# Sync loads the first keys and queries back to back, ScalarE the first values, in a new written order

## The chip, the cores and the metric

One core of a Trainium2 chip. Five instruction queues work side by side: TensorE (PE), VectorE (DVE), ScalarE (ACT), GpSimd (POOL) and sync (SP), which only issues transfers. Each runs its own queue in order. Time is device microseconds (us), median of the runs.

## What is computed

Sparse causal attention for 4 batches of 8 heads (768 positions, 64 values each), followed by a gated feed-forward layer. For each query and each chunk of 32 keys an upper bound is made from the chunk's smallest and largest key values; the six chunks with the highest bounds are kept.

```python
k_min, k_max = np.min(k_chunks, axis=3), np.max(k_chunks, axis=3)
ub = np.sum(np.maximum(q[..., None, :] * k_min, q[..., None, :] * k_max), axis=-1)
ub = np.where(causal, ub, -1e9)
top_chunks = np.argsort(ub, axis=-1)[..., -6:]
scores = np.where(sel & (i >= j), scale * q @ k.T, -1e9)
out = softmax(scores) @ v                       # (4, 8, 768, 64) -> x (3072, 512)
y = (1 / (1 + np.exp(-(x @ w_gate))) * (x @ w_val)) @ w_out   # 512 -> 1536 -> 512
```

All tensors are float32 in memory; the matmuls are in float16, besides the transposes and the bounds.

## The kernel before

The work is cut into nine stages: 128 positions of batch 0 (stage 0), the next 256 (stage 1), then seven of 384. A stage has three parts.

- Preparation: keys and queries are brought to the layout with the 64 values in partitions. For batch 0 (`prep_groups`) TensorE transposes each block of 128 positions (operations `kTp` and `qT`, line 561), DVE reduces the keys to chunk maxima and minima (`kxn`, line 571), four small DVE operations make the bounds' operand `kcat` (`kc`, lines 580 to 591), ScalarE and DVE evict the transposed keys (`hk`, line 604) and queries (`Qc`, line 522 and 526), and the queries are cast to `headQ` (`hq`, line 537). For the later batches (`prep_blocks`) DVE transposes. From stage 1 on TensorE makes the upper bounds (`ub`, line 733), and a serial chain on DVE turns them into mask rows: transpose (`ubq`, 736), causal penalty (741), the eight largest of each row (`mx`, 749), comparison (`Ap`, 754), transpose (`apT`, 757); the rows are copied beneath the queries in `headQ` (`mq`, 761), once for heads 0 to 3 and once for heads 4 to 7. Stage 0 has at most four chunks, so all are kept; it has only a guard against overflow (`ubp` line 699, guard 704 to 706, `gT` 708 and 712), and its keys and queries lie in `firstK` and `first`, with a pattern `less` copied into `firstK` (387).
- Attention: scores (`sc`, 810), exponential (`at`, 815, ScalarE), the causal triangle cut out by GpSimd (821), product with the values and a column of ones (`pv`, 835), normalisation by DVE (`xn`, 846 and 848), transpose (`xtp`, 861; `xT`, 866).
- Feed-forward: two products (`gv`, 891), `gate` on ScalarE (901), `hglu` on DVE (903), the output product (`o`, 917), its copy (`osb`, 924 or 926) and the store (932).

The order of all this is written out. The string `ORDER` names each of 1771 operations once, as kind, stage and number; `/1` or `/2` picks another of the engines that may do it. `Plan.order` walks through it with assumed durations and landings, only to find where TensorE would wait, and puts matmuls on zeros there (line 340, `fill`). On each engine the operations stand in the string's order. The same assumed times were used when the string was searched for; on the chip only the order, the engines and the number of fillers are left of them.

The first transfers stand in the table `LOADS`: lane, load, and assumed landing. The name of a load is tensor, stage and block: k10 is the keys of stage 1, block 0, 256 KB in pieces of 2 KB (line 455); v00a and v00b are the values of stage 0 for heads 0 to 3 and 4 to 7, 128 KB each in pieces of 256 B, and v10 and v11 are 256 KB each in the same pieces (line 460). Lane SP is sync's queue, Q2 is ScalarE's and Q0 is GpSimd's. `WLAND` has the assumed landings of the nine weight loads, which GpSimd issues (lines 507 and 509) with conversion to float16. GpSimd (or ScalarE) then casts the values of stages 0 and 1 into the tile `v` (line 491). p10 and p01 are copies of a pattern inside the on-chip memory (line 407). From stage 3 on keys and queries come in pieces of 128 B by sync (`kb` and `qb`, line 422).

Transfers issued by sync and ScalarE use eight completion semaphores in turn: a ninth waits until the first has landed. Six buffers are shared by all loads of keys, queries and values of this kind.

Of the kernel before, what the change touches and what calls it, by code (L numbers as in the profile page):

```python
# [20 lines left out]
ORDER = """
    c.0 kch.0 wst0.0 is.0 is.2 qch.0 c.2 w0.0 wst1.0 is.1 vn.0 c.3 vn.1 c.4 c.8/1 v.0 wst2.0 c.5 kTp:0.0 c.6 kch.1
    vn.2 qT:0.0 kxn:0.0 ps.0 kxn:0.1 Qc:0.1 qch.1 kc:0.0 wst3.0 w1.0 Qc:0.3 wst4.0 Qc:0.2 kch.2 hk:0.0 wst5.0 Qc:0.0
    hk:0.1 wst6.0 ubp:0.1 qch.2 hk:0.2/1 ubp:0.0 v.1 kTp:1.0 hk:0.3/1 c.9 qT:1.0 kxn:1.0 Ap:0.1 c.11 c.10 kxn:1.1
    Qc:1.1 wst7.0 w2.0 vn.3 gT:0.1/1 Qc:1.2/1 kTp:1.1 gT:0.0/1 sc:0.1 Qc:1.0/1 sc:0.0 at:0.2 kxn:1.3 Qc:1.3 at:0.3
    kxn:1.2 at:0.0 kc:1.0 qT:1.1 at:0.1 Qc:1.6 pl.0 hk:1.1 wst8.0 pv:0.3 pv:0.2 pv:0.6 pv:0.0 pv:0.1 Qc:1.4 xn:0.0
    w3.0 c.7 Qc:1.7 hk:1.2 xtp:0.0 pv:0.4 pv:0.7 pv:0.5 Qc:1.5 xn:0.1 hk:1.0/1 ub:1.0 Ap:0.0 xtp:0.1 ubq:1.0 hq:1.1
    xT:0.0/1 ubq:1.1 xT:0.1/1 mx8:1.0 hk:1.3/1 gv:0.6 kch.3 v.2 gv:0.0 qch.3 gv:0.7 Ap:1.0 hq:1.0/1 gv:0.1 w4.0 ub:1.1
    gv:0.8 kch.4 apT:1.0 gv:0.3 gv:0.2 gate:0.1 mq:1.3/2 v:0.0 ubq:1.2 sc:1.3 gate:0.0 mq:1.1 qch.4 ubq:1.3 at:1.6
    mx8:1.1 mq:1.0 sc:1.1 mq:1.2 gv:0.4 at:1.2 gv:0.5 Ap:1.1 sc:1.2 kch.5 at:1.4 sc:1.0 at:1.7 apT:1.1 mq:1.7/2 at:1.0  # L30
    mq:1.6/2 sc:1.7 mq:1.4/2 v.3 hglu:0.0 gv:0.9 gv:0.10 qch.5 at:1.14 sc:1.6 w5.0 at:1.3 pv:1.7 gv:0.11 at:1.1
    at:1.12 sc:1.4 at:1.5 pv:1.6 pv:1.1 mq:1.5 at:1.8 pv:1.4 pv:1.3 pv:1.2 pv:1.5 at:1.13 sc:1.5 xn:1.1 pv:1.0 at:1.9
    qT:2.0 at:1.10 at:1.15 hglu:0.1 kTp:2.0 c.13 at:1.11 xn:1.0 pv:1.14 gv:0.12 Qc:2.2 w6.0 gv:0.18 vn.4 gv:0.19
    gv:0.20 kxn:2.1 gv:0.13 c.14 gate:0.3 gv:0.14 vn.5 pv:1.9 pv:1.15 kxn:2.0 pv:1.13 gate:0.2 pv:1.10 pv:1.12 kTp:2.2
    vn.6 xn:1.3 Qc:2.0 kb:3.0 pv:1.8 pv:1.11 qT:2.2 xn:1.2 hk:2.0/1 xtp:1.0 w7.0 Qc:2.8/1 gv:0.15 Qc:2.3 gv:0.21
    xtp:1.1 xT:1.0 hk:2.1/1 gv:0.22 gv:0.23 xT:1.1 gv:0.16 gv:0.17 Qc:2.1 gv:1.0 hglu:0.2 kTp:2.1 gate:1.0 hglu:0.3
    gv:1.2 Qc:2.11 w8.0 kxn:2.2 gv:1.1 Qc:2.9 gv:1.4 hglu:1.0 gate:1.1 qT:2.1 kxn:2.5 gate:1.2 gv:1.12 Qc:2.6 kxn:2.4
    gv:1.3 gv:1.13 gate:1.6 hglu:1.1 Qc:2.5 gv:1.16 hglu:1.6 gv:1.5 kxn:2.3 gate:1.8 gv:1.10 Qc:2.10 gv:1.11 hglu:1.2
    Qc:2.4 gv:1.14 kc:2.0 gv:1.17 gate:1.5 hq:2.0 Qc:2.7 gv:1.18 hglu:1.5 hglu:1.8 gate:1.7 ub:2.0 v.4 gate:1.9 gv:1.6
    ubq:2.0 gv:1.19 kb:3.1 gate:1.3 ubq:2.1 ub:2.1 hk:2.2/1 mx8:2.0 o:0.0 kb:3.2 gv:1.7 hk:2.4/1 v.5 o:0.1 Ap:2.0  # L40
    hk:2.3/1 o:0.2 kb:3.3 o:0.3 apT:2.0 hk:2.5/1 o:0.4 mq:2.0/2 qb:3.0 v.6 o:0.5 hglu:1.9 mq:2.1 ubq:2.2 sc:2.0 mq:2.3
    gv:1.15 qb:3.1 hq:2.1 osb:0.0/1 at:2.0 sc:2.1 hglu:1.3 gv:1.20 at:2.2 qb:3.2 hglu:1.7 sc:2.3 at:2.1 ubq:2.3
    gv:1.21 mx8:2.1 gate:1.10 gv:1.8 qb:3.3 at:2.5 sc:2.2 Ap:2.1 gv:1.9 kb:3.4 gate:1.4 gv:1.22 mq:2.2 hglu:1.10
    at:2.3 sc:2.6 apT:2.1 kb:3.5 gv:1.23 gate:1.11 Qct:3.0 at:2.4 sc:2.4 at:2.9 pv:2.0 mq:2.4 kb:3.6 pv:2.4 pv:2.3
    hglu:1.4 pv:2.2 v:0.1 pv:2.1 at:2.6 sc:2.7 Qct:3.1 mq:2.5 kb:3.7 o:1.6 at:2.10 at:2.11 sc:2.5 kTt:3.0 vn:3.0
    pv:2.5 qb:3.4 o:1.7 at:2.8 xn:2.0 pv:2.11 at:2.7 sc:2.9 qb:3.5 mq:2.6 o:1.8 hglu:1.11 at:2.14 sc:2.8 mq:2.7 o:1.0
    qb:3.6 vn:3.1 at:2.12 pv:2.8 pv:2.9 pv:2.10 kTt:3.1 pv:2.7 sc:2.10 qb:3.7 rl:3.0 at:2.13 o:1.1 kn:3.0 c.12 o:1.9
    hq:3.0 kb:5.0 pv:2.6 pv:2.12 pv:2.13 at:2.15 sc:2.13 pv:2.14 kx:3.0 o:1.10 at:2.20 out:0.0 at:2.16 sc:2.12 kb:5.1
    o:1.11 at:2.18 sc:2.14 xn:2.1 o:1.2 at:2.21 o:1.3 kb:5.2 Qct:3.2 o:1.4 osb:1.1 sc:2.11 kc:3.0 o:1.5 at:2.17 kb:5.3
    sc:2.15 Qct:3.3 at:2.19 ub:3.0 at:2.23 at:2.22 pv:2.19 pv:2.17 qb:5.0 osb:1.0/1 pv:2.16 hk:3.0 pv:2.15 rl:3.1  # L50
    pv:2.20 pv:2.18 ubq:3.0 pv:2.22 pv:2.21 pv:2.23 xtp:2.0 xn:2.2 qb:5.1 hq:3.1 xT:2.0/1 xn:2.3 ubq:3.1 xtp:2.1
# [954 lines left out]
```

## Time and profile before

| | |
|---|---|
| median of 3 runs | 300.29 us (300.08 to 301.04) |
| the profiled execution | 300.8 us, span 298.8 us |
| TensorE busy | 284.5 us, 95% of the span |
| DVE, ScalarE, GpSimd busy | 71%, 68%, 36% |
| granted TensorE clock | 1.00 throughout |
| read from and written to memory | 28.31 MB and 6.29 MB |

The chain of work that ended last is TensorE for 83% of its length and DVE for 8%; 4% of the span is one transfer of queries. A row of the timeline gives start, length, engine, line, operation with its output and input, and in brackets how long the engine had been idle and what ended this. SPq and ACTq rows are the issue of a transfer, not the transfer.

### The profile page before, as it was taken

The numbers are of one execution on the slowest core, as the hardware profiler recorded it, in microseconds if no ns is written. First come the engines' busy times: TensorE is split into PE (matmuls) and PEld (weight loads), VectorE is DVE, ScalarE is ACT, GpSimd is POOL, SyncE is SP. The second block draws the span as 40 slices with busy tenths as digits, with TensorE's granted clock in tenths as the row PEclk, the third lists the DMA queues.
The fourth block names the chain that finished last, engine by engine and source line by source line (L and its number), as shares of the span: only waits on it lengthen the run. The fifth ranks groups of instructions, "written<-read, shape, count | busy, mean of one in ns | idle before, by whom it ended". The sixth has DMA issues, their size and how long they took to land.

```text
span 298.8 us, 6823 instructions
## 1 busy us (share of the span) xinstructions
PE 284.5 (95%) x2642; PEld 181.2 (61%) x2642; DVE 212.4 (71%) x581; ACT 203.9 (68%) x299; POOL 107.5 (36%) x175
## 2 busy tenths in 40 slices
PE   6668998999999999999999999999999999999995
PEld 3345983865665566566655656766665676555563
DVE  0688788998999898899988886897875434202431
ACT  3578896899786598887995886999636476331221
POOL 7567703685568143273851104326220101000000
PEclk9999999999999999999999999999999999999999
...
GB/s 152 256 218 279 229 171 114 193 149 175 74 215 160 43 141 58 96 63 109 111 85 2 124 0 2 3 3 71 20 70 2 35 2 0 2 103 39 0 70 106
DMA packets 110072, 27.99 MB, mean 94 GB/s; under 512 B 100311, under 2 KB 105525, under 8 KB 110040
## 3 DMA queue, kind: packets, MB, share of 16 engines
q1 hardware_dynamic: 81608, 19.28, 31.5%
...
q10 hardware_dynamic: 1712, 0.66, 1.1%
q8 instruction: 20, 0.33, 0.5%
q14 instruction: 12, 0.10, 0.1%
HBM read 28.31 MB, written 6.29 MB: 116 GB/s over the span
## 4 chain that ended last, share of the span: by engine, by line
PE 83%; DVE 8%; DMA 4%; ACT 2%; issue 1%; SPq 1%; DVEq 0%; ACTq 0%
PE m_o L917 21%; PE m_v L891 17%; PE m_g L891 16%; PE big_sc L810 12%; PE m_pv L835 6%; PE big_gv L891 5%; PE m_ub L733 4%; DMA ld_q<-in_q_dram 4%; PE m_xtp L861 2%; ACT Qcat L522 1%; DVE kxn L571 1%; DVE mx L749 1%; PE big_kqT L561 1%; ACT at L815 1%; DVE hglu L903 1%
## 5 line engine op out<-in xcount | busy, mean ns | idle before, releaser
L815 ACT ACTIVATE at<-big_sc 128x1024 f16<-128x1024 f32 (+3 forms) x96 | 84.7, 909 | 17.1 <-PE big_sc L810 11.6
L917 PE MATMUL m_o<-wo,hglu 128*128 128x512 f16 (+1 forms) x300 | 72.0, 370 | 0.0
L821 POOL TENSOR_SCALAR_AFFINE_SELECT at<-at 128x384 f16<-128x384 f16 (+2 forms) x66 | 33.3, 515 | 105.5 <-ACT at L815 101.6
L891 PE MATMUL m_v<-xT,wv 128*128 128x384 f16 (+2 forms) x384 | 71.2, 306 | 0.1
L891 PE MATMUL m_g<-xT,wg 128*128 128x384 f16 (+2 forms) x384 | 70.3, 306 | 0.0
L903 DVE SCALAR_TENSOR_TENSOR hglu<-gate,m_v 128x384 f16<-128x384 f16 (+1 forms) x88 | 44.9, 527 | 19.8 <-PE m_v L891 15.5
L901 ACT ACTIVATE gate<-m_g 128x384 f16<-128x384 f32 (+1 forms) x88 | 40.8, 477 | 24.4 <-PE m_g L891 20.3
L891 PEld LDWEIGHTS <-wg 128*128 128x128 f16 x432 | 38.7, 98 | 23.8 <-issue 4.4
L810 PE MATMUL big_sc<-headQ,headK 89*128 89x128 f16 (+2 forms) x472 | 51.6, 240 | 0.8 <-DVE headQ L761 0.6
L891 PEld LDWEIGHTS <-wv 128*128 128x128 f16 x432 | 38.6, 98 | 20.6 <-issue 0.9
L810 PEld LDWEIGHTS <-headK 89*128 89x128 f16 x472 | 33.4, 97 | 12.7 <-issue 1.1
L917 PEld LDWEIGHTS <-hglu 128*128 128x128 f16 x300 | 27.0, 98 | 22.7 <-issue 1.2
L835 PEld LDWEIGHTS <-at 128*128 128x128 f16 x672 | 30.2, 98 | 12.7 <-issue 1.9
L835 PE MATMUL m_pv<-v,at 128*128 128x65 f16 x672 | 34.0, 194 | 1.1 <-POOL at L821 1.1
L761 POOL COPY headQ<-apT 25x384 f16<-25x384 f16 (+1 forms) x30 | 14.7, 490 | 27.1 <-DVE apT L757 25.6
L672 DVE STREAM_TRANSPOSE Qcat<-ld_qb 64x768 f32<-64x768 f32 x24 | 23.1, 964 | 0.8 <-POOL headQ L537 0.4
L924 ACT ACTIVATE osb<-m_o 128x512 f32<-128x512 f32 (+1 forms) x17 | 9.9, 587 | 18.7 <-PE m_o L917 18.7
L903 DVE SCALAR_TENSOR_TENSOR hglu<-gate,big_gv 128x384 f16<-128x384 f16 x12 | 6.6, 553 | 21.9 <-ACT gate L901 20.7
L848 DVE TENSOR_TENSOR xnat<-m_pv,rz 128x384 f16<-128x384 f32 (+1 forms) x34 | 18.1, 534 | 1.2
L537 POOL CAST headQ<-Qcat 64x1536 f16<-64x1536 f32 (+1 forms) x11 | 15.6, 1419 | 8.8 <-ACT Qcat L522 8.6
L901 ACT ACTIVATE gate<-big_gv 128x384 f16<-128x384 f32 x12 | 5.9, 491 | 17.4 <-PE big_gv L891 17.4
L681 ACT ACTIVATE Qcat<-Qcat 64x1536 f32<-64x1536 f32 x11 | 16.3, 1483 | 0.3
...
## 6 DMA issues: line engine op xcount, KB each, us to landing
...
wv<-in_moe_w_val_dram POOLq DMA_DIRECT2D x3, 512.0 KB, 15.0
...
```

The lines of the kernel that those rows point to most:

```text
L537: copy(tl(("headQ", s), [89, H, st.n], F16)[0:64, h0:h0 + 4, :], tl(("Qcat", s))[0:64, h0:h0 + 4])
L672: nc.vector.transpose(tl(qd, [128, H, HS])[0:64, h:h + 2].rearrange("p a (c t) -> p a c t", t=CH), tl(("ld", "qb", b, u))[64 * e:64 * e + ...
L681: nc.scalar.activation(dst, src, AF.Relu)
L810: nc.tensor.matmul(ps[:, 128 * o:128 * (o + m)], (hk if s else firstK)[0:rows, h, jl:jl + 128], (tl(("headQ", s)) if s else first)[0:rows, ...
L815: add(at(x + 0.03 * t + 0.01), [("ACT", 0.19 + w * 0.815e-3, lambda sc=sc, a=a, w=w: nc.scalar.activation(tl(a, [128, 1024], F16)[:, 0:w], ...
L821: nc.gpsimd.affine_select(out=dg, in_=dg, compare_op=ALU.is_ge, fill=0.0, base=0, pattern=[[0, nd], [1, 128]], channel_multiplier=-1)
L835: nc.tensor.matmul(pvp[:, ib - q0, h % HP, :], tl(a)[:, 128 * o:128 * o + 128], head_v(b, jb // HB)[:, h, jb % HB, :], start=(jb == 0), st ...
L848: nc.vector.tensor_tensor(dst, pvp[:, :, :, 0:64], r.to_broadcast([128, nb, HP, 64]), ALU.mult)
L891: nc.tensor.matmul(ps(i)[:, n * (fb - f0):n * (fb - f0 + 1)], w16[:, c, 128 * fb:128 * fb + 128], tl(("xT", s, c // 2))[:, c % 2, :], star ...
L901: add(at(x) - EV, [("ACT", 0.18 + 0.81 * el, lambda gate=gate, ps=ps: nc.scalar.activation(tl(gate, [128, G * n], F16), ps(0), AF.Tanh, sc ...
L903: add(at(x) - EV, [("DVE", 0.15 + 1.04 * el, lambda gate=gate, hg=hg, ps=ps: nc.vector.scalar_tensor_tensor(tl(hg, [128, G * n], F16), tl( ...
L917: nc.tensor.matmul(tl(o, [128, N]), tl(("hglu", s, fc // G))[:, c0:c0 + 128], wo16[:, fc, cols], start=(fc == 0), stop=(fc == NFB - 1))
```

## The change

Two tables and the order string change, and a third table is new; `Plan.order` reads it. No operation is added or taken away.

```diff
 LATENCY = {"PE": 0.22, "ACT": 0.08, "DVE": 0.06, "POOL": 0.12, "SP": 3.0, "Q0": 3.0, "Q2": 3.0}
+BEGIN = {"DVE": 0.9, "ACT": 0.8, "POOL": 1.3}
...
-        end, eng_of, free, used, released, rings = {}, {}, {}, {}, {}, {p: [] for p in self.slots}
+        end, eng_of, free, used, released, rings = {}, {}, dict(BEGIN), {}, {}, {p: [] for p in self.slots}
...
-    WLAND = [9.6, 15.0, 18.9, 23.5, 28.6, 32.0, 35.1, 38.2, 44.6]
-    LOADS = (("SP", "k00", 4.8), ("Q2", "q00", 4.8), ("SP", "v00a", 8.0), ("Q2", "v00b", 8.0), ("SP", "k10", 10.1), ("SP", "q10", 11.7),
-             ("SP", "k11", 13.3), ("SP", "q11", 16.0), ("Q2", "v10", 17.4), ("SP", "v11", 23.8),
-             ("SP", "k20", 24.0), ("SP", "q20", 25.0), ("SP", "k21", 26.2), ("SP", "q21", 27.8), ("SP", "k22", 29.3), ("SP", "q22", 32.5),
-             ("SP", "p10", 33.7), ("SP", "p01", 35.0), ("Q0", "v20", 46.0), ("Q0", "v21", 46.5), ("Q0", "v22", 47.0))
+    WLAND = (11.7, 15.3, 19.3, 24.0, 28.5, 32.6, 35.8, 39.0, 45.4)
+    LOADS = (("SP", "k00", 4.8), ("SP", "q00", 6.1), ("Q2", "v00a", 5.0), ("Q2", "v00b", 5.5), ("SP", "k10", 8.0), ("SP", "q10", 9.4),
+             ("SP", "k11", 10.8), ("SP", "q11", 13.0), ("Q2", "v10", 13.8), ("SP", "v11", 21.2),
+             ("SP", "k20", 22.7), ("SP", "q20", 24.2), ("SP", "k21", 25.7), ("SP", "q21", 27.2), ("SP", "k22", 28.7), ("SP", "q22", 30.2),
+             ("SP", "p10", 31.4), ("SP", "p01", 32.8), ("Q0", "v20", 46.0), ("Q0", "v21", 46.5), ("Q0", "v22", 47.0))
```

The times in these tables are assumptions of the kernel's author for the planner, not measurements of this text. `ORDER` is replaced as a whole. Its beginning before and after (`wst` is the issue of a weight load, `is` an issue by ScalarE, `kch`, `qch` and `vn` loads of keys, queries and values, `c` a constant, `v:` or `v.` a cast of values):

```diff
-    c.0 kch.0 wst0.0 is.0 is.2 qch.0 c.2 w0.0 wst1.0 is.1 vn.0 c.3 vn.1 c.4 c.8/1 v.0 wst2.0 c.5 kTp:0.0 c.6 kch.1
-    vn.2 qT:0.0 kxn:0.0 ps.0 kxn:0.1 Qc:0.1 qch.1 kc:0.0 wst3.0 w1.0 Qc:0.3 wst4.0 Qc:0.2 kch.2 hk:0.0 wst5.0 Qc:0.0
...
+    kch.0 is.0 c.0 wst0.0 is.1 vn.0 qch.0 c.2 is.2 w0.0 wst1.0 kch.1 c.3 vn.1 vn.2 c.4 v.0 kTp:0.0 wst2.0 qch.1 c.5
+    kxn:0.0 qT:0.0 c.6 kch.2 kxn:0.1 Qc:0.0 c.8 qch.2 ps.0 kTp:1.0 Qc:0.2 kc:0.0 wst3.0 Qc:0.3 qT:1.0 wst4.0 Qc:0.1
...
```

What that makes of each queue at the start, in issue order:

| queue | before | after |
|---|---|---|
| sync | k00, v00a, k10, q10, k11, q11, v11, k20, ... | k00, q00, k10, q10, k11, q11, v11, k20, ... |
| ScalarE, transfers | q00, v10, v00b | v00a, v00b, v10 |
| ScalarE, then | `less` into `firstK`, 4 `Qc` of stage 0, 2 `headK` copies, 1 `Qc` of stage 1, both `gT` copies, exponentials | 4 `Qc` of stage 0, 4 `Qc` of q10, 1 `gT` copy, both exponentials, 4 `Qc` of q11 |
| DVE | `kxn`, `kc`, `hk` of stage 0, guard, 2 `kxn`, 2 `Qc`, 2 `kxn`, `kc`, `hk` | `kxn`, `less`, `kc`, `hk` of stage 0, guard, `kxn`, 1 `gT` copy, 3 `kxn`, `hk`, `kc`, `hk` |
| GpSimd | ..., wg, wv, wg, wv (third), wo, cast of v00, ..., wo, masks of stage 0, wo | ..., wv, wg (third), cast of v00, wv (third), memset, 2 `headK` copies and the pattern `pen` with a wo issue between, masks of stage 0, wo, wo |
| TensorE | k00, q00, fillers, `ubp`, k10, q10, `gT`, k11, scores, q11, `pv` | k00, q00, k10, q10, `ubp`, k11, `gT`, q11, scores, fillers, `pv` |

In the whole program TensorE has 13 fillers fewer. On GpSimd the two `headQ` casts of stage 2 (line 537) stand directly behind each other, where mask-row copies stood between; the two of stage 1 are both on ScalarE. Behind stage 2 the order has the same structure, with heads and blocks exchanged here and there and some copies on another of the three engines.

More of the change, by code (lines that the diff above doesn't have):

```diff
@@ L25 @@
[L25 to L49, printed above, removed]
@@ new lines @@
+    ubq:4.0 kb:7.3 o:2.8 ubq:4.1 o:2.9 mx8:4.0 pv:3.23 o:2.10 o:2.11 Ap:4.0 pv:3.20 pv:3.21 pv:3.5 osb:2.1 pv:3.4
+    ub:4.1 apT:4.0 pv:3.19 pv:3.3 pv:3.22 pv:3.18 out:2.1 o:2.12 ubq:4.2 mq:4.0/1 pv:3.0 pv:3.2 pv:3.1 o:2.13 out:2.0
+    mq:4.1/1 xn:3.3 o:2.14 mq:4.2/1 sc:4.1 xn:3.0 xtp:3.1 at:4.2 o:2.15 ubq:4.3 mx8:4.1 xtp:3.0 sc:4.0 xT:3.1/1 o:2.16
+    kTt:5.0 xT:3.0/1 o:2.17 sc:4.3 Ap:4.1 osb:2.2 gv:3.4 gv:3.5 at:4.0 out:2.2 gv:3.6 kTt:5.1 gv:3.8 qb:7.0 gv:3.9
+    gate:3.1 sc:4.4 apT:4.1 at:4.5 gv:3.7 Qct:5.1 mq:4.5 gv:3.16 gv:3.17 qb:7.1 hk:5.0 mq:4.3/1 sc:4.2 hglu:3.1
```

208 lines of the change are left out of this document (114 added, 94 removed).

## The prediction

> **What bounds the kernel now.** I read the page's busy table, then TensorE's busy time by stretch, then the same for its filler matmuls alone (line 340, on zeros), then the first 50 us of the timeline.
>
> ```profile
> PE 284.5 (95%) x2642; PEld 181.2 (61%) x2642; DVE 212.4 (71%) x581; ACT 203.9 (68%) x299; POOL 107.5 (36%) x175
> 0.00:30.00 30.00, 21.30 (x169) 1.00 1.07 227
> 30.00:45.00 15.00, 14.68 (x200) 1.00 1.37 197
> 45.00:50.00 5.00, 3.60 (x33) 1.00 0.93 105
> 60.00:291.00 231.00, 230.54 (x2116) 1.00 0.44 65
> 0.00:30.00 30.00, 11.23 (x45) 4.46 (x45) 1.00 1.07 227
> ```
>
> The columns of a stretch are its length, busy time (instructions), granted clock, DMA share and GB/s; the last row is filler alone. TensorE is the bound: 284.5 us of 298.8, never throttled (1.00). Of its busy time 11.23 us is filler, all before 30 us. Time without useful matmuls: 30 - (21.30 - 11.23) = 19.9 us before 30 us, 0.3 us from 30 to 45, 1.4 us from 45 to 50, 0.5 us in the 231 us from 60 to 291. Useful work is the same in both kernels, so a gain can only come out of the 19.9 and the 1.4, and a loss can arise anywhere. The next rows show what the 19.9 us waits for.
>
> ```profile
> 4.24 1.04 ACT L387 COPY firstK<-less 8x1024 f16<-8x1024 f16 x1 [0.19 <-POOL less L368]
> 5.82 0.54 SPq L455 DMA_DIRECT2D ld_q<-in_q_dram  x1
> 6.82 1.06 PE L561 MATMUL m_qT<-ident,ld_q 128*128 128x128 f32 x4
> 7.06 1.29 DVE L571 TENSOR_REDUCE kxn<-m_kT 128x32 f32<-128x512 f32 x2 [5.83 <-PE m_kT L561]
> 7.92 2.99 ACT L522 ACTIVATE first<-m_qT 64x512 f16<-64x512 f32 x4 [2.64 <-PE m_qT L561]
> 9.38 1.46 DVE L604 CAST firstK<-m_kT 64x512 f16<-64x512 f32 x2
> 10.11 0.76 POOL L507 DMA_DIRECT2D wv<-in_moe_w_val_dram  x1
> 10.87 1.14 ACT L611 COPY headK<-firstK 64x512 f16<-64x512 f16 x2
> 11.48 0.19 DVE L704 TENSOR_TENSOR over<-m_ub,pen 128x32 f32<-128x32 f32 x1 [0.65 <-PE m_ub L699]
> 11.71 0.95 SPq L455 DMA_DIRECT2D ld_k<-in_k_dram  x1
> 12.80 0.66 PE L561 MATMUL big_kT<-ident,ld_k 128*128 128x128 f32 x4 [1.36 <-DMA ld_k<-in_k_dram]
> 14.45 0.66 PE L561 MATMUL big_qT<-ident,ld_q 128*128 128x128 f32 x4 [0.98 <-DMA ld_q<-in_q_dram]
> 14.94 0.27 PE L708 MATMUL m_gT<-ident,guard 128*8 128x128 f32 x1
> 15.66 1.03 ACT L712 CAST first<-m_gT 8x512 f16<-8x512 f32 x2
> 15.68 0.42 PEld L561 LDWEIGHTS big_kT<-ident,ld_k 128*128 128x128 f32 x4 [0.53 <-DMA ld_k<-in_k_dram]
> 16.26 0.86 PE L810 MATMUL m_sc<-first,firstK 72*128 72x128 f16 x8
> 16.71 0.60 ACT L815 ACTIVATE at<-m_sc 128x512 f16<-128x512 f32 x1
> 17.07 0.54 SPq L455 DMA_DIRECT2D ld_k<-in_k_dram  x1
> 17.19 0.62 POOL L491 CAST v<-ld_v 128x512 f16<-128x512 f32 x1 [5.57 <-DMA ld_v<-in_v_dram]
> 18.41 0.30 DVE L580 COPY kmx<-kxn 64x128 f32<-64x128 f32 x1
> 18.65 0.60 PE L561 MATMUL big_qT<-ident,ld_q 128*128 128x128 f32 x4
> 19.28 1.25 ACT L522 ACTIVATE Qcat<-big_qT 64x512 f32<-64x512 f32 x2 [0.71 <-PE big_qT L561]
> 19.37 1.25 POOL L821 TENSOR_SCALAR_AFFINE_SELECT at<-at 128x512 f16<-128x512 f16 x2
> 20.15 0.60 DVE L591 TENSOR_TENSOR kcat<-kmx,kcat 64x64 f32<-64x64 f32 x1
> 20.68 0.33 PE L835 MATMUL m_pv<-v,at 128*128 128x65 f16 x5 [1.10 <-POOL at L821]
> 20.77 0.74 DVE L604 CAST headK<-big_kT 64x512 f16<-64x512 f32 x1
> 22.90 0.42 DVE L848 TENSOR_TENSOR xnat<-m_pv,rz 128x256 f16<-128x256 f32 x1
> 23.68 0.45 DVE L736 STREAM_TRANSPOSE ubq<-m_ub 128x256 f32<-128x256 f32 x1 [0.36 <-PE m_ub L733]
> 29.29 1.19 DVE L761 COPY headQ<-apT 25x256 f16<-25x256 f16 x3
> 44.89 1.46 POOL L537 CAST headQ<-Qcat 64x1536 f16<-64x1536 f32 x1 [8.60 <-ACT Qcat L522]
> 44.89 1.63 DVE L591 TENSOR_TENSOR kcat<-kmx,kcat 64x96 f32<-64x96 f32 x1
> 47.12 0.85 PE L733 MATMUL m_ub<-Qcat,kcat 128*32 128x384 f32 x8 [1.40 <-DVE hglu L903]
> ```
>
> A row is start, length, engine, line, operation and, in brackets, the idle time before it and who ended it. I name a load by letter, stage and block (k10 is keys, stage 1, block 0). Three waits stand in it. Stage 1's keys and queries land at 12.80 (k10), 14.45 (q10), 15.68 (k11), and stage 0's small transpose (m_gT) stands in TensorE's queue behind q10's: its guard was ready at 12.1. GpSimd waits 5.57 us for the second half of v00, to 17.19, and its masks of stage 0 (19.37) and stage 0's value products (20.68) come behind that. And DVE's serial mask chain of stage 1 runs from 23.68 to 30.48; only then can the last four heads' scores start.
>
> **The change, part by part.**
>
> *Loads.* Sync loses v00a and gains q00; ScalarE loses q00 and issues v00a, v00b, v10 in that order, where it issued q00, v10, v00b. Every load from SP or ACT takes one of eight semaphores in turn, so sync's q11 waits for k00: that dates k00's landing at 5.82. Behind it one 256 KB block of k or q took 1.65 us (12.80 to 14.45) and 1.23 us (to 15.68); I take 1.45. From 5.8 that gives q00 7.3, k10 8.7, q10 10.1, k11 11.6, q11 13.0. In the kernel before, q11 is then 15.68 + 1.45 = 17.1 (by 18.65 at the latest, when it is transposed). So stage 1's blocks come about 4 us earlier, because v00a's 512 pieces of 256 B no longer stand in sync's queue between k00 and k10.
>
> A rule of the Trainium skill speaks against this. "DMA: Bandwidth & Descriptors", section "Issuing engines are not separate DMA queues", says that transfers from sync, ScalarE and GpSimd run on the same 16 DMA engines and interleave, so that another issuer saves only issue time. By it the bytes ahead of q11 are what they were and q11 stays near 17.1; the sum would be the first rival's. The rows lean the other way: between 12.80 and 15.68 sync's queue got 512 KB while v00b, 128 KB on ScalarE's, crept on from about 11.7 to 17.19.
>
> *v00 and GpSimd.* v00a and v00b are now first on ScalarE's queue. One bound: v10, 256 KB in the same pieces and behind q00, was there by 11.71 (the issue of k20 at 11.71 waits for it). The other: v00b alone took 17.19 - 11.71 = 5.5 us, so two such take 11 us and, if they begin at about 2 (an estimate, 1.2 after the first issue), land at 13. I take 11.5, range 9 to 13. The cast now stands behind wg's third load and ahead of wv's (10.11), so GpSimd waits 1.4 us there, not 5.57. Queued behind it: cast 0.62, wv 0.76, a memset 0.41, two copies of headK that came from ScalarE (0.57 each there; 0.62 by the cast of the same size), the pen pattern 0.45, one wo issue 0.77. GpSimd reaches stage 0's masks at 11.5 + 4.2 = 15.7.
>
> *Stage 0.* q00's transposes at 7.3 to 8.4, ScalarE's four evictions 2.99 to 11.4. The copy of "less" moves from ScalarE to DVE: 1.04 by its row, at least 0.5 by the half of L712's 1.03. DVE: 7.06 + 1.29 + 1.04 + 1.09 (bounds) + 1.46 = 11.95, guard 0.62 to 12.6, half a microsecond later than now. But m_gT now stands behind k11 (11.6), not q10's 14.45, and runs at 12.7. Its two copies, 0.51 each by L712: DVE after one reduction (0.65, half of L571's row) by 13.8, ScalarE after four evictions of q10 (0.62 each by the row at 19.28, so 2.5 from 11.4) by 14.4. q11's transposes now stand ahead of the scores on TensorE, a new wait: 13.0 to 13.7, hidden. Scores from 13.8, exponentials 0.60 each to 15.5, masks 15.7 to 16.95, value products 17.0 against 20.68. With v00 at 13 it would be 18.5.
>
> *Stage 1's mask chain.* DVE from 13.8: three reductions 1.95, headK 0.74, bounds 2.34 (18.41 to 20.77), headK 0.74, one normalisation 0.63 (0.42 and a reciprocal of about 0.2): 20.2 against 23.68. ScalarE's four evictions of q11 end at 15.5 + 2.5 = 18.0, in time. The other normalisation now stands between the two halves, 0.63 more, so the chain ends at 27.6 against 30.48: 2.9 us earlier; between this and the 3.5 of its start I take **3.0**. ScalarE takes stage 1's second headQ cast over from GpSimd (about 1.0) and has from 18.0 on for it, beside the chain. The bounds operation is held by GpSimd's work in places: 0.60 at 20.15. Without that, 1.5 us more; the same hold-up kept, none. I keep it.
>
> *Later.* What is late next? wv's last third landed at 34.0 and is first used at 36.56; the new order puts 1.7 us more matmuls ahead of it, so it is wanted at 35.3, still after the landing.
>
> ```profile
> 36.56 0.61 PE L891 MATMUL m_v<-xT,wv 128*128 128x128 f16 x8
> DMA to landing us min/median/max: 23.9/23.9/23.9
> ```
>
> (The landing counts from the issue at 10.11.) Stage 2's loads come earlier with sync's queue: k21 waited at 17.07 for v00b, and now for v10. The 1.4 us at 45 to 47 is DVE's bounds operation held for 1.63 us beside GpSimd's 1.46 us cast, with TensorE's m_ub behind it. The new order issues both casts there back to back, so the hold-up may be gone (1.4 gained), the same, or one cast longer (1.46 lost); nearest is the same, and I charge 0.3. The order from 60 us on is new too; the old one lost 0.46 us in 231, and I take the same. The last copies of the output end the same way in both orders, at nothing.
>
> Sum on the profiled execution: 300.8 with a span of 298.8; 298.8 - 3.0 + 0.3 = 296.1. Its time stands 0.5 above the median of 300.29, so the median becomes 300.3 - 2.7 = **297.6 us**; with the bounds above (4.4 gained, or 1.2) 295.9 to 299.1.
>
> **Rivals.**
> First, slower: q11 lands as late as before. For it: the DMA share is above 1 throughout, the bytes ahead are the same. Against it: the pace of sync's own queue (1.45 us a block). Its place is TensorE's queue, where q11's transposes now stand ahead of stage 0's scores. With q11 at 17.1 the scores start at 17.8 (16.26 before), the masks end at 20.2, q11's evictions at 22.0, so m_ub of stage 1 comes about where it was: 300.3, no change. Each microsecond beyond about 17.5 is lost in full; at 18.65 the evictions end 1.6 later, and with the extra 0.63 in the chain the kernel takes 300.6 to 302, say 301.3.
> Second: both casts hold the bounds operation. DVE waits 2.9, TensorE 2.86 instead of 1.40: the gain is 1.5, 298.8. For it: the two casts are adjacent on GpSimd; against: the first starts only when ScalarE's last query copy ends, and DVE may be past it.
> Third, faster still: the bounds operation is free both times: 3.0 + 1.5 + 1.4 gained, 294.4. Against it: both rows (20.15 and 44.89) stand beside GpSimd work, and GpSimd has as much to do there in the new order.
>
> **How the numbers follow.** A measurement of this kernel tells 0.3% (0.9 us) from no change. Forecast 0.52; second rival 0.12; third 0.07; q11 late without loss 0.11; q11 late with loss 0.18. Faster: 0.52 + 0.12 + 0.07 = 0.71; same 0.11; slower 0.18. The range runs from 295.3 to 301.0: it leaves out most of the third (0.05) and the worse half of the slower case (0.1).
>
> **What would show it.** Right: k10, q10, k11 transposed before 12 us; the cast of v00 before 13; m_gT at about 12.7; value products of stage 0 near 17; ubq of stage 1 near 20; filler and idle before 30 us down from 19.9 to about 17. Wrong: scores of stage 0 waiting for a DMA of q, GpSimd waiting for v00 past 15, DVE's bounds operation of stage 2 above 2 us with TensorE idle behind it, or new idle time of TensorE after 60 us, which no row of the kernel before can show.

## The result, and the profile after

The changed kernel takes 304.22 us (median of 4 runs, 302.17 to 304.95) where the kernel before takes 300.19 (4 runs, 300.08 to 301.04): 1.011 times the time, 95% interval 1.0079 to 1.0141. It is slower; 297.6 was predicted, and the range ended at 301.0. The profiled execution takes 304.9 us, its span is 303.2 (before: 298.8).

Busy times and the granted clock by slice, from the page of the changed kernel:

```profile
PE 286.3 (94%) x2629; PEld 182.5 (60%) x2629; DVE 211.5 (70%) x577; ACT 200.6 (66%) x297; POOL 111.3 (37%) x181
...
PEclk9797995999999999999999999999999999999999
```

TensorE is busy 1.8 us longer than before, with 13 fillers fewer; the clock, 1.00 throughout in the profiled execution before, dips in three slices (7, 7 and 5 tenths). TensorE by stretch (length, busy, granted clock, DMA share, GB/s), and last the filler alone (line 341 here):

```profile
0.00:30.00 30.00, 20.47 (x168) 0.89 1.09 233
30.00:45.00 15.00, 14.39 (x188) 1.00 1.36 186
45.00:60.00 15.00, 12.74 (x87) 0.77 1.11 164
60.00:291.00 231.00, 230.16 (x2140) 1.00 0.44 65
0.00:30.00 30.00, 8.52 (x32) 3.33 (x32) 0.89 1.09 233
```

In what follows, *lost time* of a stretch is its length less useful work, and useful work is busy time without filler, times the granted clock, summed over steps of 0.25 us of this view. Line numbers are one higher than before (bounds operation L592, `m_ub` L734, casts L538). To 30 us the kernel before loses 19.9 us and the changed one 20.4, of it 2.4 by half clock; from 45 to 60 us it is 1.4 before and 5.2 after, namely 15 - 12.74 = 2.26 of idle time and 2.98 of half clock. From 30 to 45 us it is 0.6 against 0.3, from 60 to 291 us 231 - 230.16 = 0.84 against 0.46. So the loss sits between 45 and 60 us, beside a gain that is missing before 30; the order behind 60 us has little part in it. The sum of these differences is 5.0, the spans differ by 4.4; the method is good to about a microsecond.

The timeline rows that answer to those of the prediction:

```profile
8.32 0.65 PE L562 MATMUL m_qT<-ident,ld_q 128*128 128x128 f32 x4 [2.51 <-DMA ld_q<-in_q_dram]
9.94 1.12 PE L562 MATMUL big_kT<-ident,ld_k 128*128 128x128 f32 x4
10.16 0.62 POOL L492 CAST v<-ld_v 128x512 f16<-128x512 f32 x1
11.70 0.88 PE L562 MATMUL big_qT<-ident,ld_q 128*128 128x128 f32 x4
13.78 0.27 PE L709 MATMUL m_gT<-ident,guard 128*8 128x128 f32 x1
18.44 0.42 PE L836 MATMUL m_pv<-v,at 128*128 128x65 f16 x8 [0.67 <-POOL at L822]
18.89 0.27 DVE L592 TENSOR_TENSOR kcat<-kmx,kcat 64x64 f32<-64x64 f32 x1
23.44 0.42 DVE L849 TENSOR_TENSOR xnat<-m_pv,rz 128x256 f16<-128x256 f32 x1
23.93 0.28 PE L862 MATMUL m_xtp<-ident,xnat 128*128 128x128 f16 x2 [2.43 <-DVE xnat L849]
25.09 0.83 PE L892 MATMUL m_g<-xT,wg 128*128 128x128 f16 x12
26.26 0.83 DVE L762 COPY headQ<-apT 25x256 f16<-25x256 f16 x3
44.03 2.91 POOL L538 CAST headQ<-Qcat 64x1536 f16<-64x1536 f32 x2 [7.85 <-ACT Qcat L523]
44.11 1.51 DVE L591 TENSOR_TENSOR kmx<-kxn,kmx 64x96 f32<-64x96 f32 x1
45.65 1.47 DVE L592 TENSOR_TENSOR kcat<-kmx,kcat 64x96 f32<-64x96 f32 x1
47.26 1.51 PE L734 MATMUL m_ub<-Qcat,kcat 128*32 128x384 f32 x8 [2.87 <-DVE kcat L592]
```

Up to the row at 18.89 the events come in the predicted order, mostly 1 to 2 us later than predicted and 1 to 3 us earlier than before. The mask chain of stage 1 ends at 27.1 instead of 30.48. But the first feed-forward product (`m_g`) comes at 25.09; before it came at 24.56:

```profile
24.56 1.06 PE L891 MATMUL m_g<-xT,wg 128*128 128x128 f16 x16
```

The feed-forward of stage 0 needs both halves of its normalised values, and the new order has the second (xnat at 23.44) behind the first half of the mask chain on DVE, where the old one had it at 22.90, ahead of the chain. At 25 us the two kernels have lost the same, 18.8 and 18.7 us. Then, around 44 us, GpSimd runs its two casts without a pause, DVE's bounds operation beside them ends at 47.1, and the wait for it is the longest of all (waits of TensorE: in total, times, longest):

```profile
PE m_ub L734 <- DVE kcat L592: 2.9, 1, 2.9
PE m_xtp L862 <- DVE xnat L849: 2.8, 2, 2.4
PE m_qT L562 <- DMA ld_q<-in_q_dram: 2.5, 1, 2.5
```

Behind each of these three idle times comes a stretch at a clock of 0.50. Stretches of 3.41 us, in which the last three rows belong to the third idle time:

```profile
5.44:8.85 3.41, 0.90 (x8) 1.00 1.14 244
8.85:12.26 3.41, 3.29 (x13) 0.50 1.16 284
12.26:15.68 3.42, 2.04 (x20) 1.00 1.20 230
...
19.09:22.50 3.41, 2.10 (x24) 1.00 1.17 247
22.50:25.92 3.42, 1.67 (x25) 1.00 1.15 275
25.92:29.33 3.41, 3.41 (x34) 0.50 1.16 267
...
42.98:46.40 3.42, 1.41 (x13) 1.00 0.91 96
46.40:49.81 3.41, 2.55 (x14) 0.50 0.79 93
49.81:53.22 3.41, 3.41 (x20) 0.50 1.12 179
```

### The profile page after: what moved, and what is told of

Same layout as the page of the kernel before. It is cut to its first block, busy times and chain, and to the rows that moved or that the text cites. A ratio compares the mean times of both kernels' runs of the same rounds, so it can differ in the third digit from the quotient of the medians.

```text
span 303.2 us, 6802 instructions
## 1 busy us (share of the span) xinstructions
PE 286.3 (94%) x2629; PEld 182.5 (60%) x2629; DVE 211.5 (70%) x577; ACT 200.6 (66%) x297; POOL 111.3 (37%) x181
## 4 chain that ended last, share of the span: by engine, by line
PE 89%; ACT 3%; DMA 3%; DVE 2%; issue 1%; SPq 0%; POOL 0%; DVEq 0%; ACTq 0%
PE m_o L918 20%; PE m_g L892 19%; PE m_v L892 18%; PE big_sc L811 12%; PE m_pv L836 7%; PE big_gv L892 5%; PE m_ub L734 4%; DMA ld_k<-in_k_dram 3%; ACT Qcat L523 2%; PE m_xtp L862 2%; ACT at L816 1%; PE big_kqT L562 1%; DVE kcat L592 0%; PE big_qT L341 0%; DVE kmx L591 0%
## 5 line engine op out<-in xcount | busy, mean ns | idle before, releaser
L816 ACT ACTIVATE at<-big_sc 128x896 f16<-128x896 f32 (+3 forms) x96 | 84.7, 909 | 16.4 <-PE big_sc L811 11.4
L918 PE MATMUL m_o<-wo,hglu 128*128 128x512 f16 (+1 forms) x300 | 73.2, 370 | 0.0
L892 PE MATMUL m_v<-xT,wv 128*128 128x384 f16 (+2 forms) x384 | 72.7, 310 | 0.0
L892 PE MATMUL m_g<-xT,wg 128*128 128x384 f16 (+2 forms) x384 | 71.4, 313 | 0.4 <-ACT gate L902 0.3
L892 PEld LDWEIGHTS <-wg 128*128 128x128 f16 x432 | 40.1, 101 | 24.0 <-issue 3.9
L836 PEld LDWEIGHTS <-at 128*128 128x128 f16 x672 | 31.3, 98 | 13.1 <-issue 1.2
L762 POOL COPY headQ<-apT 25x384 f16<-25x384 f16 (+1 forms) x34 | 16.7, 491 | 37.6 <-DVE apT L758 34.7
L538 POOL CAST headQ<-Qcat 64x1536 f16<-64x1536 f32 x11 | 16.0, 1463 | 16.9 <-DVE Qcat L673 9.0
L925 ACT ACTIVATE osb<-m_o 128x512 f32<-128x512 f32 x17 | 10.2, 597 | 18.3 <-PE m_o L918 18.1
L904 DVE SCALAR_TENSOR_TENSOR hglu<-gate,big_gv 128x384 f16<-128x384 f16 x12 | 6.6, 554 | 20.0 <-ACT gate L902 19.9
L734 PE MATMUL m_ub<-Qcat,kcat 128*32 128x384 f32 (+1 forms) x128 | 14.7, 522 | 3.3 <-DVE kcat L592 2.9
## 6 DMA issues: line engine op xcount, KB each, us to landing
ld_k<-in_k_dram SPq DMA_DIRECT2D x6, 256.0 KB, 10.1
```

The costliest lines, as they stand in the source:

```text
L734: nc.tensor.matmul(ps[32 * i:32 * i + 32, :], kcat[:, 4 * u + i, :], tl(("Qcat", s))[:, 4 * u + i, :], start=True, stop=True)
L762: copy(tl(("headQ", s), [89, H, st.n], F16)[64:89, h, :], tl(apT)[32 * i:32 * i + 25, :])
L816: add(at(x + 0.03 * t + 0.01), [("ACT", 0.19 + w * 0.815e-3, lambda sc=sc, a=a, w=w: nc.scalar.activation(tl(a, [128, 1024], F16)[:, 0:w], ...
L836: nc.tensor.matmul(pvp[:, ib - q0, h % HP, :], tl(a)[:, 128 * o:128 * o + 128], head_v(b, jb // HB)[:, h, jb % HB, :], start=(jb == 0), st ...
L892: nc.tensor.matmul(ps(i)[:, n * (fb - f0):n * (fb - f0 + 1)], w16[:, c, 128 * fb:128 * fb + 128], tl(("xT", s, c // 2))[:, c % 2, :], star ...
L904: add(at(x) - EV, [("DVE", 0.15 + 1.04 * el, lambda gate=gate, hg=hg, ps=ps: nc.vector.scalar_tensor_tensor(tl(hg, [128, G * n], F16), tl( ...
```

## The experiments

Theories: the half clock behind idle time costs the 4 us (clock theory); the two adjacent casts hold DVE's bounds (hold theory); and for the missing gain at 30 us, theory F (the start of stage 0's feed-forward is what counts) against theory C, the prediction's (the end of the mask chain counts). In a table, for each kernel: median and the median of the kernel before on the same chip, ratio with interval, span of the profiled execution, and from its trace lost time to 30 us, lost time from 45 to 60 us, and start of the first feed-forward product. The changed kernel was not timed again beside the later runs: it is compared through the kernel before, which took 300.1 to 300.2 us beside the changed kernel, e1 to e4 and e12, and 300.8 to 300.9 us beside e5 to e11.

| kernel | us | before | ratio | span | lost to 30 | lost 45-60 | first m_g |
|---|---|---|---|---|---|---|---|
| before | | | | 298.8 | 19.9 | 1.4 | 24.56 |
| changed | 304.22 | 300.19 | 1.0110 (1.0079-1.0141) | 303.2 | 20.4 | 5.2 | 25.09 |
| e1 fillers | 300.65 | 300.13 | 1.0021 (1.0003-1.0038) | 300.7 | 20.8 | 2.7 | 26.92 |
| e2 casts on ScalarE | 301.80 | 300.13 | 1.0051 (1.0030-1.0073) | 301.2 | 22.3 | 1.8 | 27.04 |
| e3 both | 300.21 | 300.13 | 1.0003 (0.9989-1.0016) | 298.9 | 20.0 | 1.1 | 26.06 |
| e4 before, no fillers | 300.24 | 300.13 | 0.9998 (0.9983-1.0013) | 298.2 | 21.0 | 0.1 | 23.49 |
| e5 feed-forward first | 302.86 | 300.90 | 1.0051 (1.0024-1.0079) | 303.6 | 20.8 | 5.4 | 24.56 |
| e6 the same, casts apart | 300.93 | 300.90 | 1.0002 (0.9981-1.0022) | 298.9 | 19.0 | 0.4 | 23.00 |
| e7 casts apart | 301.69 | 300.90 | 1.0019 (0.9997-1.0040) | 300.1 | 20.5 | 0.6 | 26.19 |
| e8 loads alone | 300.25 | 300.90 | 0.9982 (0.9964-1.0000) | 298.4 | 17.6 | 0.0 | 21.93 |
| e9 loads, one cast moved | 300.39 | 300.85 | 0.9986 (0.9970-1.0002) | 297.9 | 18.4 | 0.0 | 22.30 |
| e10 e8, xn late | 301.68 | 300.85 | 1.0026 (1.0002-1.0051) | 300.1 | 21.7 | 0.1 | 25.91 |
| e11 e9, keys first | 300.62 | 300.78 | 0.9981 (0.9967-0.9994) | 301.2 | 18.1 | 0.4 | 22.78 |
| e12 one place filled | 302.97 | 300.06 | 1.0106 (1.0081-1.0132) | 300.1 | 20.2 | 2.1 | 24.69 |

The medians of e2, e5, e7 and e12 lie 0.2 to 0.4 us above the range expected of the theory that their traces bear out; beside e5 and e7 the kernel before itself took 0.7 us more. e3, e6 and e8 missed the gain in time that was hoped for and came where their second expectation had them, at 300 or more.

### The clock: e1, e12, e4

e1 puts fillers into the three idle times, e12 only into the last:

```diff
+EXTRA = {"qT:0.0": 8, "xtp:0.0": 36, "ub:2.0": 16}     # e12: {"ub:2.0": 16}
...
+                if plan.kinds[i][1][1:] in EXTRA:
+                    fill(EXTRA[plan.kinds[i][1][1:]], plan.tasks[i][5](True))
                 if plan.tasks[i][1][o][2]:
                     plan.tasks[i][1][o][2]()
```

> The changed kernel with 60 more filler matmuls on zeros in front of three operations before which TensorE stood idle: 8 of 512 columns before q00's transposes (2.51 us idle), 36 of 128 before the second xnat transpose (2.43 us), 16 of 384 before stage 2's bounds (2.87 us). Clock theory (the 4 us lost are matmuls at half clock that follow these idle times): the granted clock is 1.00 all through, the idle times keep their length but are filled, and the time falls by the four half-clock stretches of 3.41 us, about 0.9 to 1.1 each, to 300.3 (299.8 to 300.8). Rival (the new order itself costs the time, the low clock falls where TensorE waits anyway): 303.5 to 304.5, whatever the clock.

> The changed kernel with 16 fillers in front of stage 2's bounds alone, in the wait of 2.87 us behind the two casts, which stays as long as it was. It prices the half clock behind that wait by itself: the other idle times, before q00's transposes and before the second xnat transpose, are left. Clock theory: no half clock between 45 and 55 us, lost time between 45 and 60 us 2.5 to 3.0 instead of 5.24, time 1.5 to 3.0 us under the changed kernel's, 301.3 to 302.8 where the kernel before takes 300.2 to 300.9. If the half clock there costs nothing, or comes elsewhere: 303.5 to 305.

TensorE from 45 to 60 us, in e1 and in e12 (the same view as above):

```profile
45.00:60.00 15.00, 14.60 (x128) 1.00 0.95 138
```

```profile
45.00:60.00 15.00, 14.59 (x140) 1.00 1.08 160
```

In both the clock stays at 1.00 there, the casts still hold the bounds (1.47 us each time), and 2.5 to 3.1 us less are lost than in the changed kernel's trace. e1's median is 0.5 us above that of the kernel before, the changed kernel's 4.0: matmuls that compute nothing win back 3.5 us. The rival, that the order itself takes these 3.5 us, falls. Its clock was not 1.00 throughout as expected (0.989 in the profiled execution, where it dipped between 12 and 20 us; 0.998 to 1.00 in the nine others). e12 is not as clear: its profiled execution, 301.83 us, was the fastest of four, the others took 302.87 to 303.62, and the ratio is the changed kernel's. So the stretch at 46.4 costs 3 us in the trace that has it, but the medians, 2.9 above the kernel before against 4.0, show about 1 us for it and the ratios none; how often it comes, four runs of each don't tell. The rest of what e1 gains (1.0106 to 1.0021) comes with the fillers in the two earlier gaps, which were not tried apart.

> The kernel before without the 38 fillers that the planner puts behind 5.5 us (the 7 at the start stay). Clock theory: TensorE then idles over long stretches between 6 and 28 us, the granted clock falls to 0.50 in three to six stretches of 3.41 us, and the time rises by about 1 us for each, to 303 (301.5 to 305). Rival (fillers only take time on the path): clock 1.00 and 300.3 or less.

e4 is the kernel before without the fillers behind 5.5 us:

```diff
-                if ps is not None:
+                if ps is not None and False:
```

```profile
0.00:30.00 30.00, 18.08 (x127) 0.66 1.07 225
```

In the profiled execution the clock falls as foreseen, to 0.56 on average from 5 to 25 us, over 20 us in all. But it costs next to nothing: lost time to 30 us is 1.1 higher, and the median is that of the kernel before (its span of 298.2 has another 1.4 us to its credit, the hold at stage 2 that it was spared; see the last section). Of its ten runs three had a mean clock of 0.964 or 0.965 and took 299.98, 300.39 and 300.60 us; five had 1.00 and took 300.02 to 300.67. The expectation of 303 was wrong. The kernel before shows the same without any edit: of its 29 runs beside e1 to e4, 12 had a clock of 1.00 and a median of 300.59 us, and 17 had 0.983 to 0.998 and a median of 300.04. As these runs read, half clock costs where TensorE is what the rest waits for, and before 25 us it mostly is not. The stretch at 8.85 in the changed kernel is therefore hardly a cause of its loss; the one at 25.92 can be, since dense work has begun.

### The casts: e2, e7, e3

```diff
-Qc:2.5 hq:2.0 hglu:1.7 ... gv:1.18 hq:2.1 hk:2.3/1 kb:3.3
+Qc:2.5 hglu:1.7 ... gv:1.18 hk:2.3/1 hq:2.0/1 hq:2.1/1 kb:3.3                          # e2, and e3 with fillers
+Qc:2.5 hglu:1.7 ... gv:1.18 hk:2.3/1 hq:2.0/1 kb:3.3 ... mq:2.3/1 mq:2.2 hq:2.1         # e7
```

> The changed kernel with both headQ casts of stage 2 given to ScalarE behind its last two headK copies, so that GpSimd does nothing beside DVE's bounds operations. Hold theory (the two casts side by side hold DVE's bounds, and the wait of 2.87 us behind them brings two half-clock stretches): m_ub of stage 2 waits 0.9 to 1.0 us instead of 2.87, the half clock after 46.4 is gone while those before 12 and 30 us stay, time 304.2 - 2.0 - 1.9 = 300.3 (299.5 to 301.5). Rival (the wait is DVE's own work and not the casts): m_ub still waits over 2.5 us, time 303.5 to 304.5.

> The changed kernel with the casts of the run above and nothing else. Hold theory: m_ub of stage 2 waits under 1.2 us instead of 2.87, the half clock at 46.4 to 53.2 is gone, ScalarE's gate copies wait for one cast only, not for two; lost time between 45 and 60 us under 1.5 instead of 5.2, time 300 to 301.3 (301.8 with both casts on ScalarE).

> Both edits, with 5 fillers instead of 16 before stage 2's bounds. If both theories hold: clock 1.00, m_ub of stage 2 at about 45.3, 304.2 - 3.9 - 2.0 = 298.3 (297.6 to 299.0), faster than both kernels. If the early gain is lost for another reason: 300 or more.

Waits of TensorE in e2, and then in e7:

```profile
PE m_o L918 <- ACT gate L902: 1.2, 1, 1.2
...
PE m_ub L734 <- DVE kcat L592: 0.5, 1, 0.5
```

```profile
PE m_ub L735 <- DVE kcat L593: 0.5, 1, 0.5
```

The bounds operation takes 0.32 us instead of 1.47 in all three, the wait of 2.87 us shrinks to 0.46 in e2 and e7, and the half clock from 46.4 to 53.2 is gone: the hold theory holds. With both casts on ScalarE a gate copy comes late and 1.2 us go elsewhere; e7, with one, has no such wait. e3 was expected at 298.3 and took 300.21. With clock and casts mended, the new order is level with the old, no faster: the predicted gain at 30 us (lost 20.0 against 19.9) is not there even so.

### Where the early gain went: e5, e6, e8, e10

e5 moves stage 0's second normalisation ahead of the chain, and the feed-forward products with it; e6 adds e7's casts:

```diff
-xn:0.1 hk:1.0/1 ub:1.0 ... ubq:1.0 xtp:0.1 pl.0 ... xT:0.1/1 qch.3 ... apT:1.0 v.2 xn:0.0 ... ubq:1.2 xtp:0.0 mq:1.2 xT:0.0/1
+xn:0.1 xn:0.0 hk:1.0/1 ub:1.0 ... ubq:1.0 xtp:0.1 xtp:0.0 pl.0 ... xT:0.1/1 xT:0.0/1 qch.3 ... apT:1.0 v.2 ... ubq:1.2 mq:1.2
-sc:1.1
+gv:0.6 gv:0.7 gv:0.8 gv:0.0 gv:0.1 gv:0.2 gv:0.3 gv:0.4 sc:1.1
```

> The changed kernel, but stage 0's second normalisation moved on DVE from behind the first half of the mask chain to directly ahead of it, its transpose and copy with it, and eight feed-forward products of stage 0 moved on TensorE ahead of the first scores of stage 1. The mask chain of stage 1 starts 0.6 us later than in the changed kernel and ends no earlier. Theory F (TensorE's dense work begins with stage 0's feed-forward, so what counts is when its input is transposed, 24.6 us in the changed kernel): first feed-forward product at 22.5 to 23 instead of 25.09, no idle time of 2.43 us, TensorE's lost time (length minus busy time without filler, times the clock) at 30 us down from 20.4 by 1.5 to 3, no half clock at 25.9; time 300.5 to 302.5, with the loss behind 45 us still in it. Theory C (the prediction's: the end of the mask chain sets the time): lost time at 30 us the same or up to 0.6 more, time 304 to 305.

> The edit of the run above, and stage 2's first headQ cast on ScalarE behind two headK copies, its second on GpSimd behind a mask-row copy. Theory F with the hold theory: lost time at 30 us 17.5 to 19, m_ub of stage 2 waits under 1.2 us, clock 0.99 to 1.00, time 297.5 to 299.0, faster than both kernels. If the early part cannot be shortened: 300 or more.

In e5's profiled execution the loads of stage 1 came so much later (stage 0's `m_pv` at 20.06, not 18.44) that its lost time to 30 us, 20.8, says nothing; the idle time of 2.43 us and the half clock at 25.9 are gone. e6, with `m_pv` at 18.27, can be held against the changed kernel's trace: first product at 23.00, 2.1 earlier, and lost time to 30 us 1.4 less, short of the 17.5 to 19 that was expected by a hair. From e7, timed on the same chip, it differs by the early edit alone: median 0.8 less, the intervals overlapping. Its median was to be 297.5 to 299.0 and is that of the kernel before.

e8 is the cleaner test: the loads of the change in the order before, in which the normalisations stand ahead of the chain.

```diff
-c.0 kch.0 wst0.0 is.0 is.2 qch.0 c.2 w0.0 wst1.0 is.1 vn.0
+c.0 kch.0 wst0.0 is.0 is.1 qch.0 c.2 w0.0 wst1.0 is.2 vn.0
```

(`LOADS` and `WLAND` are the changed kernel's.)

> The kernel before with the changed loads alone: the tables of the changed kernel, and ScalarE issuing v00a, v00b, v10; the order is the old one in all else. The prediction's step on the loads: k10, q10, k11 transposed 3 us or more earlier, stage 0's products with the values at 17 to 18. Theory F: stage 0's normalisations, which the old order has ahead of the mask chain, come earlier too, first feed-forward product at 21.5 to 23.5 instead of 24.56, lost time at 30 us down from 19.9 by 1 to 2.5, time 298 to 299.3. If the gain of the loads is taken by waits of the old order: 300.

```profile
21.93 1.05 PE L891 MATMUL m_g<-xT,wg 128*128 128x128 f16 x16
...
44.42 0.85 PE L733 MATMUL m_ub<-Qcat,kcat 128*32 128x384 f32 x8 [1.40 <-DVE hglu L903]
```

First product 2.6 us earlier, lost time to 30 us 2.3 less, and stage 2's bounds at 44.42 instead of 47.12, 2.7 earlier: what the prediction had expected of the change up to here, the loads alone do. The median, 300.25 us, shows little of it, which e9 follows up. e10 then takes e8 and puts the second normalisation behind half of the chain, as the changed kernel has it, and behind it the products that need it:

```diff
-Qc:1.5 xn:0.1 hk:1.0/1 ub:1.0 Ap:0.0 xtp:0.1 ubq:1.0 ... xT:0.1/1 ... gv:0.6 kch.3 v.2 gv:0.0 qch.3 gv:0.7 Ap:1.0 ... gv:0.1 w4.0 ub:1.1 gv:0.8 kch.4 apT:1.0
+Qc:1.5 hk:1.0/1 ub:1.0 Ap:0.0 ubq:1.0 ... kch.3 v.2 qch.3 Ap:1.0 ... w4.0 ub:1.1 kch.4 apT:1.0 xn:0.1 xtp:0.1 xT:0.1/1 gv:0.6 gv:0.0 gv:0.7 gv:0.1 gv:0.8
```

> The kernel before with the changed loads, but stage 0's second normalisation moved on DVE from ahead of the mask chain of stage 1 to behind its first half, as in the changed kernel, its transpose and copy behind it, and the feed-forward products that need it moved behind the second bounds product on TensorE. The mask chain is not delayed by this. Theory F: the first feed-forward product comes at 24.5 to 25.5 instead of 21.93, TensorE idles over 2 us before it, lost time at 30 us 19.5 to 21.5 instead of 17.6, time 1.5 to 3.5 us over that of the loads alone. Theory C: the chain's end decides, and the time is that of the loads alone or less.

```profile
25.46 0.29 PE L859 MATMUL m_xtp<-ident,xnat 128*128 128x128 f16 x2 [2.70 <-DVE xnat L846]
...
25.91 2.27 PE L889 MATMUL m_g<-xT,wg 128*128 128x128 f16 x24
```

This gives the changed kernel's picture: idle 2.70 us, the first product at 25.91, half clock behind it, lost time to 30 us 21.7. Of the 4.0 us between the two products 1.2 are this execution's later loads (`m_pv` 19.46 for 18.21), the rest is the move. All of the loads' gain is gone; the ratio goes from 0.9982 to 1.0026, 1.4 us in the medians. Theory F stands; the mask chain's end does not decide: in e10 it comes at 28.8, 1.7 us earlier than in the kernel before, and yet 1.8 us more are lost to 30 us. The time from stage 0's first value product (`m_pv`) to the first feed-forward product, which does not hang on when the loads land, says the same: 3.9 us before, 3.7 in e8, 6.7 in the changed kernel, 6.5 in e10.

### What takes the rest: e9, e11

e8 gains 2.7 us up to 44 us, but its span is only 0.4 shorter. In the order before, the same products can be followed; for e8 and e9, where stage 2's first cast is on ScalarE (`hq:2.0` behind `Qc` becomes `hq:2.0/1` behind `gate:1.9`), their start against the kernel before:

| bounds product (`m_ub`) | before | e8 | e9 |
|---|---|---|---|
| stage 2, first | 47.12 | -2.70 | -3.66 |
| stage 3, first | 70.11 | -1.81 | -2.35 |
| stage 3, second | 73.64 | -1.29 | -1.83 |
| stage 4, first | 95.72 | -1.28 | -1.83 |
| stage 4, second | 100.17 | -0.42 | -0.97 |
| stage 8, last | 224.29 | -0.44 | -0.99 |

> The kernel before with the changed loads, and stage 2's first headQ cast on ScalarE behind a gate copy instead of on GpSimd beside DVE's bounds. Hold theory: the bounds operation of stage 2 takes 0.2 to 0.4 us instead of 1.6, m_ub waits under 0.3 us instead of 1.40, and with the 0.6 us that the loads alone gained the time is 1.0 to 2.0 us under that of the kernel before, clock 1.00, faster than both kernels. If the gain is given back at stage 3's bounds, where the loads alone already lost 0.8 us: the same as the loads alone, 0.3 to 0.9 under the kernel before.

Keys of stage 3 and its bounds, before and then in e9:

```profile
61.69 0.97 DVE L641 STREAM_TRANSPOSE kT_kT<-ld_kb 128x768 f32<-128x768 f32 x1
...
70.11 0.85 PE L733 MATMUL m_ub<-Qcat,kcat 128*32 128x384 f32 x8
```

```profile
61.33 0.98 DVE L641 STREAM_TRANSPOSE kT_kT<-ld_kb 128x768 f32<-128x768 f32 x1 [3.21 <-DMA ld_kb<-in_k_dram]
...
67.76 1.18 PE L733 MATMUL m_ub<-Qcat,kcat 128*32 128x384 f32 x8 [1.23 <-ACT at L815]
```

e9's edit does its part (stage 2's bounds wait no more, 1 us gained on e8), and then the other of its two expectations comes true, that the gain is given back at stage 3's bounds: DVE waits 3.21 us for stage 3's keys, which land at 61.3 although everything else is 3 us ahead, and the bounds wait behind them. The floor was there before, where the same operation came at 61.69 without a wait; the new order has one too (in e6 the operation waits 1.21 us for its keys, to 60.38, and TensorE idles 1.4 us from 60 to 75 us, 0.4 before). Why the keys land then was not looked into. At the next step, stage 4, e8 loses 0.86 by another hold of DVE beside GpSimd (last section). e11 lets sync load all of stage 3's keys ahead of its queries.

```diff
-for u in range(2):
-    for i, (src, n) in enumerate(((k, "kb"), (q, "qb"))):
+for u, i in (((0, 0), (1, 0), (0, 1), (1, 1)) if b == 1 else ((0, 0), (0, 1), (1, 0), (1, 1))):
+    for src, n in (((k, "kb"), (q, "qb"))[i],):
```

In the string `qb:3.0` to `qb:3.3` change places with `kb:3.4` to `kb:3.7`, and the places of `Qct:3.0 Qct:3.1 kTt:3.0 kTt:3.1 rl:3.0 kn:3.0 kx:3.0` are taken by `kTt:3.0 kTt:3.1 kn:3.0 kx:3.0 Qct:3.0 Qct:3.1 rl:3.0`.

> The kernel of the run with the loads and one cast on ScalarE, and stage 3's second four key loads issued by sync ahead of its first four query loads; DVE transposes and reduces the keys first and the queries after them. Theory L (what is gained before 50 us is given back at stage 3's bounds because the second half of its keys lands at 61.3 us, whatever comes before): second kT transpose at 57 to 58.5 instead of 61.3, m_ub of stage 3 waits under 0.5 us instead of 1.23, lost time at 75 us 19.2 to 19.8 instead of 20.4, time 1.0 to 2.0 us under that of the kernel before. If the queries, now later, take the place of the keys: the wait stays at about 1.2 us and the time 0.3 to 0.6 under.

```profile
56.36 0.98 DVE L643 STREAM_TRANSPOSE kT_kT<-ld_kb 128x768 f32<-128x768 f32 x1 [1.36 <-issue]
...
66.91 0.55 PE L812 MATMUL big_sc<-headQ,headK 89*128 89x128 f16 x6 [2.25 <-ACT at L817]
```

The keys come 5 us earlier and the bounds no longer wait for them, but another wait takes their place: 2.25 us, on ScalarE's exponentials, which stand behind the copy of the queries that now come late. The profiled execution (302.95 us) was the slowest of thirteen. The ratio, 0.9981 with its interval just below 1, is the lowest of all, by less than a measurement of 0.3% tells. No version clearly beats the kernel before.

## Why the prediction was wrong

*Loads: right in kind, somewhat too early.* k10, q10 and k11 were transposed at 9.94, 11.70 and 13.22: 2.5 to 2.9 us earlier than before, and 1.2 to 1.6 later than their predicted landings. v00's cast came at 10.16 without a wait (range 9 to 13); the landing itself was far off, since v00b had landed by 5.2 us (1.25 and 3.9 from issue to landing) and only GpSimd's queue held its cast. e8 shows 2.7 us from the loads at 44 us. The first rival fell: q11 was transposed at 15.62, not kept at 17.1 or later. The rule weighed there from the Trainium skill, "DMA: Bandwidth & Descriptors", section "Issuing engines are not separate DMA queues", does not fall with it. Both the prediction and that rival took the bytes ahead of q11 to be unchanged, and they are not: v10's 256 KB landed at 11.6 us before (issued at 1.51, 10.1 to landing) and land at 16.8 now (1.80 and 15.0), behind q11; ScalarE now issues them last. e8 has this exchange too, so no run tells v00a's move out of sync's queue, which the prediction named as the cause, from v10's move to the end of ScalarE's. q00 came 1.0 later than predicted (8.32 for 7.3), and stage 0 with it: `m_gT` 13.78 for 12.7, value products 18.44 for 17.0.

*Stage 1's mask chain: the step that failed first.* Its end was predicted 2.9 us earlier and came 3.4 earlier, partly by luck: stage 0 came more than a microsecond late, and the bounds ahead of the chain, charged at 2.34 us with the old hold kept, took 1.12 (18.04 to 19.16). But "I take 3.0" counted this in full as TensorE's time. The kernel before has no room for that behind its first feed-forward product at 24.56. Its TensorE from 25 to 30 us, and the filler in it:

```profile
25.00:30.00 5.00, 4.23 (x60) 1.00 1.14 284
25.00:30.00 5.00, 0.38 (x1) 0.10 (x1) 1.00 1.14 284
```

It loses 5 - (4.23 - 0.38) = 1.15 us there and 0.3 from 30 to 45, so an earlier end of the chain can give back 1.5 at most. A larger gain needs that product earlier. The queues were read for the chain and not for the second normalisation, which the new order puts behind half of it; the text even noted that it stands "between the two halves" and charged 0.63 to the chain, nothing to what waits for it. The runs show 2.4 to 2.7 us of idle TensorE in front of that transpose instead (2.43 in the changed kernel, 2.70 in e10). e10 reproduces the loss by that move, e8 shows the gain without it.

*Later: the casts.* "Nearest is the same, and I charge 0.3" was wrong; the second rival, given 12%, came true in its waits, though not in its time of 298.8, which kept the 3.0: TensorE waits 2.87 (2.86 predicted), DVE is held for 1.51 in the operation ahead (44.11) and 1.47 in this one (45.65). The argument against it, that DVE may be past it when the first cast starts, had no row behind it: in the kernel before the two start in the same hundredth, at 44.89.

*What no step had: the clock.* "Never throttled (1.00)" was read as a property of the kernel; it was one of its profiled execution, and 17 of 29 later runs had less. That 13 fillers fewer are to blame is not shown: e4, with 38 fewer, took no longer. In the changed kernel's trace 1.7 us go to half clock from 25.9 to 29.3 and 2.98 from 46.4 to 53.2. e2 and e7, without the wait at 47 and the half clock behind it, are 1.7 and 0.8 us above the kernel before where the changed kernel is 4.0: 2.4 and 3.2 us for the wait and the half clock together.

*What is late next: one floor was missed.* The weights were named; the keys of stage 3, at 61.7 with hardly any room, were not. In the old order they alone hold an early gain to about 2 us at 70 us (e8: 1.8, e9: 2.35). By lost time the miss is: to 30 us 20.4 instead of 16.9, from 45 to 60 us 5.2 instead of 1.7.
